# First x chunk turned on TensorE from a plain load, and wk spread over two queues, in place of DMA transposes for every x chunk and wk on one queue

## The chip, the cores and the metric

The kernel runs on one core of one Trainium2 chip. The metric is the device time of one execution in microseconds, the median of three runs. The profile is that of one execution, and its own time is given beside its span.

## The reference

Inputs are x (2048 rows of 640, bfloat16), the weights of two branches, and a gate vector. Branch A is a linear attention with 32 heads of 20, branch B a mixer with shifted groups and an MLP. The two are mixed row by row.

```python
def _A_ref(x, wqkv, wo):
    qkv = (x @ wqkv) split into q, k, v of 32 heads x 20
    phi = lambda t: jnp.where(t > 0, t + 1, jnp.exp(t)) + 1e-6
    pq, pk = phi(q), phi(k)
    kv = jnp.einsum("bhsd,bhse->bhde", pk, v)
    z = jnp.einsum("bhsd->bhd", pk)
    num = jnp.einsum("bhqd,bhde->bhqe", pq, kv)
    den = jnp.einsum("bhqd,bhd->bhq", pq, z)[..., None] + 1e-6
    return (num / den) in rows of 640 @ wo

def _B_ref(x, w1, w2, w3, w4):
    h = _gelu(_layernorm(x) @ w1)
    hs = (four column groups of h shifted by 1, -1, 2, -2 rows) @ w2
    x1 = x + hs
    return x1 + _gelu(_layernorm(x1) @ w3) @ w4

g = _sigmoid((x * gate_w).sum(-1, keepdims=True))
out = g * a + (1 - g) * b
```

## The kernel before

The 2048 rows are 16 chunks of 128 (NCH), or 4 tiles of 512 (NT). The 640 columns are 5 slices of 128 (DC). The order of work on every engine is the program's order: the kernel is written out by hand in stages, and no scheduler moves anything.

The stages in order: K (`k_mm`, `k_evac`, lines 184 to 221), one chunk at a time, 5 slices by 2 halves of the columns; Q (`q_unit`, L228); G, the product of phi(k) with x (`g_unit`, L303), with the statistics and scaling of the first layernorm on VectorE; the first B product (`w1_unit`, L337), the attention's small matrices, den (L239 to L250); then, tile by tile, the second B product (L408), attention (L439), w3 (L455) and w4 (L472).

K needs x transposed: `xT` holds x with its columns on the partitions, 5 slices by 2048. Before the change all of it is made by DMA transposes straight from memory (`load_xT`, L121), eight of them, on SP's queue, for chunks 0, 1, 2, 3, 4-5, 6-7, 8-11 and 12-15. Behind them on the same queue stand the loads of wq, of the untransposed `x_sb` (`load_x`, L118) and of all other weights. K's weights `wk_sb` come in 5 slices of 128 rows (`load_wk`, L124), 160 KB each, all on ACT's queue, with the small gate vector `g5` (L128) behind the first.

The column 640 of `wk_sb` is the gate vector: it arrives as 5 rows of 128, is turned on TensorE (L206) and copied by VectorE (L207), so that K's second half gives the gate's logit as a 321st column.

TensorE begins with products of ones (`warmup`, L200), first 6 of 512 columns and 2 of 128, then g's transpose, then 4 of 128. K's first two chunks are interleaved so that each slice of wk is used by both: chunk 0 takes slices 0, 1, 2, each followed by a product of ones of 256 columns; chunk 1 takes slices 0, 1, 2; then both take slice 3, then slice 4. From chunk 2 on each chunk takes its five slices in a row.

`k_evac` copies the gate's logit on ACT (L192) and forms phi: exp on ACT (L180), then two instructions on VectorE (L181, L182) that write `pk`.

PSUM is one pool of four buffers of two banks each (`pair`). A K chunk takes one, and so do the products of ones together with g's transpose.

Of the kernel before, what the change touches and what calls it, by code (L numbers as in the profile page):

```python
# [9 lines left out]
BF16 = mybir.dt.bfloat16  # L10
# [6 lines left out]
def kernel(  # L17
# [13 lines left out]
    nc = tc.nc  # L31
    P = 128
    S, D = A_x.shape[1], A_x.shape[2]
    F = B_w3.shape[1]
    H, Dh = 32, 20
    NCH = S // P
# [3 lines left out]
    DC = D // P  # L40
    HD = D // 2
# [27 lines left out]
    def pair():  # L69
        return ps.tile([P, 2, 512], F32, name="pp")  # L70


    x_sb = const.tile([P, NCH, D + 2], BF16)
# [12 lines left out]
    ident = const.tile([P, P], BF16)  # L86
    g5 = const.tile([DC, P], BF16)
# [19 lines left out]
    wk_sb = st1.tile([P, DC, D + 16], BF16)  # L107
    gT = wk_sb
    xT = st1.tile([P, DC, S], BF16)
# [5 lines left out]
    sp, aq, gq = nc.sync, nc.scalar, nc.gpsimd  # L115

    def load_x(c0, c1):
        sp.dma_start(x_sb[:, c0:c1, 0:D], x2[c0 * P:c1 * P, :].rearrange("(c p) d -> p c d", p=P))  # L118

    def load_xT(c0, c1):  # L120
        sp.dma_start_transpose(xT[:, :, c0 * P:c1 * P], x2[c0 * P:c1 * P, :])  # L121

    def load_wk(q, dc):
        q.dma_start(wk_sb[:, dc, 0:D], A_wqkv[dc * P:(dc + 1) * P, D:2 * D])  # L124

    load_wk(aq, 0)
    load_xT(0, 1)
    aq.dma_start(g5[:], gate_w.rearrange("(c p) -> c p", p=P))  # L128
    for dc in range(1, DC):
        load_wk(aq, dc)  # L130
    for c0, c1 in ((1, 2), (2, 3), (3, 4), (4, 6), (6, 8), (8, 12), (12, 16)):
        load_xT(c0, c1)
    sp.dma_start(wq_sb, wqkv_v[:, :, 0:D])
    load_x(0, 8)
    load_x(8, 12)
    load_x(12, 16)
    sp.dma_start(wv_sb[:], wqkv_v[:, :, 2 * D:3 * D])
# [37 lines left out]
    def phi(dst, src, n):  # L175
        e = e_p.tile([P, 1024], BF16, name="e")
        ev = e[:, 0:n]
        if len(src.shape) == 3:
            ev = ev.rearrange("p (h e) -> p h e", h=src.shape[1])
        nc.scalar.activation(ev, src, ACT.Exp)  # L180
        nc.vector.tensor_scalar(e[:, 0:n], e[:, 0:n], 1.0, 1e-6, op0=ALU.min, op1=ALU.add)  # L181
        nc.vector.scalar_tensor_tensor(dst, src, 0.0, ev, op0=ALU.max, op1=ALU.add)  # L182

    def k_mm(pt, c, dcs, hfs=(0, 1), last=DC - 1):
        for dc in dcs:
            for hf in hfs:
                n = HD + hf
                nc.tensor.matmul(pt[:, hf, 0:n], lhsT=xT[:, dc, c * P:(c + 1) * P],  # L188
                                 rhs=wk_sb[:, dc, hf * HD:hf * HD + n], start=(dc == 0), stop=(dc == last))

    def k_evac(pt, c):
        nc.scalar.copy(ylog[:, c:c + 1], pt[:, 1, HD:HD + 1])  # L192
        phi(pk[:, c, :].rearrange("p (h e) -> p h e", h=2), pt[:, :, 0:HD], D)
# [4 lines left out]
    def warmup(n, w=TS):  # L198
        for i in range(n):
            nc.tensor.matmul(warm[:, 1, 0:w], lhsT=one[:, 0:P], rhs=one[:, 0:w], start=True, stop=True)  # L200

    warmup(6)
    warmup(2, P)
    kp = [pair(), pair()]
    tg = warm[:, 0, :].bitcast(BF16)
    nc.tensor.transpose(tg[:, 0:DC], g5[:], ident[0:DC, 0:DC])  # L206
    nc.vector.tensor_copy(wk_sb[:, :, D], tg[:, 0:DC])  # L207
    warmup(4, P)
    for dc in range(3):
        k_mm(kp[0], 0, (dc,))  # L210
        warmup(1, 2 * P)
    k_mm(kp[1], 1, (0, 1, 2))
    for c in range(2):
        k_mm(kp[c], c, (3,))
    for c in range(2):
        k_mm(kp[c], c, (4,))
        k_evac(kp[c], c)
    for c in range(2, NCH):
        pt = pair()
        k_mm(pt, c, range(DC))  # L220
        k_evac(pt, c)
# [364 lines left out]
```

## Time and profile before

| | |
|---|---|
| time before, median of 3 runs | 268.53 us (268.37 to 268.89) |
| the profiled execution's own time | 268.89 us |
| its span, first to last instruction | 267.2 us |
| granted TensorE clock, mean | 0.997 |
| TensorE busy | 260.6 us (98%) |
| K stage from 9.35 to 29.13 us | 144 of its 160 products |

Times inside the profile count from the start of its span. In the page's first part each engine has its busy time, its share of the span and the number of its instructions. The chain of waits lists, in order of time, the work that the end depended on: start, length, and what it was. In the timeline a line is a run of like instructions: start, length, engine, line, operation, what it writes and reads, how many; in brackets the idle time of the engine before it and what ended it. A line of the DMA view gives what is moved, the queue that issues it, how many, their size, and the time from issue to landing. Matmul ends are modelled, so the step from one start to the next tells more than a single length.

### The profile page before, as it was taken

To read this page: it belongs to the slowest core of one execution; us is meant where nothing else is said; L and a number is where in the kernel's file an instruction comes from. 1 tells how busy PE (TensorE), PEld (TensorE's weight loads), DVE (VectorE), ACT (ScalarE), POOL (GpSimd) and SP (SyncE) were. 2 spreads that over 40 slices of the span, in tenths; PEclk is the share of its full clock that TensorE was granted. 3 is DMA by queue.
4 is the path that set the end of the run, shared out by engine and by line. 5 is a ranking of instruction groups with operands and counts; after the bars stand their busy time and mean duration, and the time that the engine had idled before them with its cause. 6 is when DMAs were issued, how large, how long until landed. Compare 5 with 4: busy or idle time off the path is not lost.

```text
span 267.2 us, 4246 instructions
## 1 busy us (share of the span) xinstructions
PE 260.6 (98%) x1738; PEld 162.2 (61%) x1738; DVE 138.5 (52%) x268; ACT 84.2 (32%) x122; POOL 20.4 (8%) x55
## 2 busy tenths in 40 slices
PE   7899999999999999999999999999999999999994
PEld 3677655688854654556567556567565566455662
DVE  0398778799948497864502464503454413122032
ACT  1455444411164716713330212340222340333100
POOL 7100010012220041001000001000001000000000
PEclk9999999999999999999999999999999999999998
DMA  7999988016676125800042000042000042000011
GB/s 147 210 209 367 374 258 319 0 27 123 123 96 125 29 42 98 305 2 0 15 86 76 25 0 2 0 98 76 25 0 2 1 98 76 25 0 2 0 61 37
DMA packets 46748, 23.77 MB, mean 89 GB/s; under 512 B 36106, under 2 KB 46090, under 8 KB 46730
## 3 DMA queue, kind: packets, MB, share of 16 engines
q1 hardware_dynamic: 46000, 22.70, 32.8%
q10 hardware_dynamic: 730, 0.82, 1.4%
q8 instruction: 13, 0.21, 0.3%
q14 instruction: 5, 0.04, 0.0%
HBM read 12.21 MB, written 2.62 MB: 56 GB/s over the span
## 4 chain that ended last, share of the span: by engine, by line
PE 92%; DMA 4%; DVE 2%; issue 0%; ACTq 0%; DVEq 0%
PE pp L472 21%; PE pp L455 21%; PE pp L303 8%; PE pp L408 8%; PE pp L439 8%; PE pp L228 8%; PE pp L188 7%; PE pp L337 6%; DMA wk_sb<-in_A_wqkv_dram 2%; DVE r_bf L250 1%; PE pp L460 1%; DMA lnxT<-ln 1%; PE pp L481 1%; PE pp L375 1%; DMA g<-in_gate_w_dram 1%; DVE hsT L347 0%
## 5 line engine op out<-in xcount | busy, mean ns | idle before, releaser
L455 PE MATMUL pp<-lnxT,w_sb 128*128 128x512 bf16 x260 | 60.4, 379 | 0.0
L463 ACT ACTIVATE h<-pp 128x1024 bf16<-128x1024 f32 (+1 forms) x28 | 27.8, 993 | 102.8 <-PE pp L455 94.4
L472 PE MATMUL pp<-w_sb,h 128*128 128x320 bf16 x416 | 57.9, 299 | 0.0
L472 PEld LDWEIGHTS <-h 128*128 128x128 bf16 x416 | 40.1, 98 | 17.0 <-issue 1.9
L455 PEld LDWEIGHTS <-w_sb 128*128 128x128 bf16 x260 | 25.4, 98 | 26.7
L488 DVE SCALAR_TENSOR_TENSOR oc<-pp,omg,x 128x640 bf16<-128x640 f32 x15 | 12.9, 881 | 44.0 <-PE pp L481 27.1
L442 DVE SCALAR_TENSOR_TENSOR x<-pp,gate,x 128x640 f32<-128x640 f32 x16 | 13.9, 868 | 29.4 <-PE pp L439 29.4
L411 DVE TENSOR_TENSOR x<-pp,x_sb 128x640 f32<-128x640 f32 x16 | 13.1, 820 | 22.9 <-PE pp L408 22.9
L180 ACT ACTIVATE e<-pp 128x640 bf16<-128x640 f32 (+1 forms) x26 | 21.5, 828 | 9.6 <-PE pp L228 9.6
L439 PE MATMUL pp<-m_sb,pqT 128*128 128x320 bf16 x160 | 24.3, 299 | 0.0
L188 PE MATMUL pp<-wk_sb,xT 128*128 128x320 bf16 (+1 forms) x160 | 23.1, 304 | 1.2 <-DMA wk_sb<-in_A_wqkv_dram 1.2
L408 PE MATMUL pp<-w_sb,hsT 128*128 128x320 bf16 x160 | 23.9, 299 | 0.0
L303 PE MATMUL pp<-x_sb,pk 128*128 128x320 bf16 (+1 forms) x160 | 22.3, 300 | 0.0
L228 PE MATMUL pp<-xT,hsT 128*128 128x512 bf16 x100 | 21.7, 379 | 0.0
L303 PEld LDWEIGHTS <-pk 128*128 128x128 bf16 x160 | 18.8, 117 | 3.5
L188 PEld LDWEIGHTS <-xT 128*128 128x128 bf16 x160 | 15.8, 99 | 7.9 <-issue 1.7
L408 PEld LDWEIGHTS <-hsT 128*128 128x128 bf16 x160 | 15.6, 98 | 8.2 <-issue 0.2
L439 PEld LDWEIGHTS <-pqT 128*128 128x128 bf16 x160 | 15.7, 98 | 7.7
L337 PE MATMUL pp<-lnxT,w_sb 128*128 128x512 bf16 x80 | 17.9, 379 | 0.0
L228 PEld LDWEIGHTS <-hsT 128*128 128x128 bf16 x100 | 11.8, 118 | 9.7
L273 POOL TENSOR_SCALAR rstd<-mv 128x4 f32<-128x4 f32 (+1 forms) x11 | 3.4, 313 | 157.2 <-DVE mv L279 157.2
L181 DVE TENSOR_SCALAR e<-e 128x640 bf16<-128x640 bf16 (+1 forms) x26 | 9.6, 368 | 11.2 <-ACT e L180 10.3
(73 smaller groups left out, 192.4 us busy)
## 6 DMA issues: line engine op xcount, KB each, us to landing
out_dram<-oc SPq DMA_DIRECT2D x15, 160.0 KB, 1.8
w_sb<-in_B_w_dram SPq DMA_DIRECT2D x1, 2160.0 KB
w_sb<-in_B_w_dram SPq DMA_DIRECT2D x1, 2080.0 KB, 10.3
x_sb<-in_A_x_dram SPq DMA_DIRECT2D x1, 1280.0 KB, 8.6
x_sb<-in_A_x_dram SPq DMA_DIRECT2D x2, 640.0 KB, 10.5
wo_sb<-in_A_wo_dram SPq DMA_DIRECT2D x6, 160.0 KB, 7.6
wk_sb<-in_A_wqkv_dram ACTq DMA_DIRECT2D x5, 160.0 KB, 3.8
hsT<-in_A_wqkv_dram SPq DMA_DIRECT2D x1, 800.0 KB, 5.6
```

Source lines behind the costliest of these rows:

```text
L180: nc.scalar.activation(ev, src, ACT.Exp)
L188: nc.tensor.matmul(pt[:, hf, 0:n], lhsT=xT[:, dc, c * P:(c + 1) * P], rhs=wk_sb[:, dc, hf * HD:hf * HD + n], start=(dc == 0), stop=(dc == ...
L228: nc.tensor.matmul(pt[:, t % 2, :], lhsT=wq_sb[:, dc, :].rearrange("p (m j) -> p j m", j=DC)[:, j], rhs=xT[:, dc, t * TS:(t + 1) * TS], st ...
L303: nc.tensor.matmul(pt[:, hf, 0:HD + hf], lhsT=w, rhs=x_sb[:, c, hf * HD:(hf + 1) * HD + hf], start=(c == 0), stop=(c == NCH - 1))
L337: nc.tensor.matmul(pt[:, i, :], lhsT=w, rhs=lnxT[t][:, dc, :], start=(dc == 0), stop=(dc == DC - 1))
L408: nc.tensor.matmul(pt[:, hf, 0:HD], lhsT=hsT[:, fc, 2 + c * P:2 + (c + 1) * P], rhs=w2_sb[:, fc, hf * HD:(hf + 1) * HD], start=(fc == 0), ...
L411: nc.vector.tensor_tensor(x1[:].rearrange("p (h e) -> p h e", h=2), pt[:, :, 0:HD], x_sb[:, c, 0:D].rearrange("p (h e) -> p h e", h=2), op ...
L439: nc.tensor.matmul(pt[:, hf, 0:HD], lhsT=pqT[:, j, c * P:(c + 1) * P], rhs=m_sb[:, j, hf * HD:(hf + 1) * HD], start=(j == 0), stop=(j == D ...
L442: nc.vector.scalar_tensor_tensor(x1, pt[:, :, 0:HD], gate[:, c:c + 1], x1, op0=ALU.mult, op1=ALU.add)
L455: nc.tensor.matmul(pt[:, k, :], lhsT=w3_sb[:, dc, fc * P:(fc + 1) * P], rhs=lnT[:, dc, :], start=(dc == 0), stop=(dc == DC - 1))
L463: nc.scalar.activation(h2[:, 2 * i * TS:2 * i * TS + n], pt[:].rearrange("p h e -> p (h e)")[:, 0:n], ACT.Gelu_apprx_tanh)
L472: nc.tensor.matmul(dst, lhsT=st[t]["h2"][:, fc * TS + cc * P:fc * TS + (cc + 1) * P], rhs=w4_sb[:, fc, a:b], start=start and fc == 0, stop ...
```

## The change

x chunk 0 is no longer transposed by DMA. It is loaded plainly into `x_sb`, first on SP's queue, and turned on TensorE in five transposes, two into one PSUM buffer and three into another; VectorE copies them into `xT`. g's transpose and copy stand between the two groups. The later `load_x(0, 8)` becomes `load_x(1, 8)`.

wk's slices 1 and 3 go on SP's queue, ahead of the DMA transposes; g, then slices 0, 2 and 4 on ACT's.

The products of ones ahead are 5 of 512 and 1 of 128 columns instead of 6 and 2; those behind g's copy are 5 of 128 instead of 4. K's chunk 0 is worked alone, its slices in the order 1, 0, 2, 3, 4, with a product of 256 columns of ones after each but the last; chunk 1 is worked like all later ones.

```diff
-    load_wk(aq, 0)
-    load_xT(0, 1)
-    aq.dma_start(g5[:], gate_w.rearrange("(c p) -> c p", p=P))
-    for dc in range(1, DC):
-        load_wk(aq, dc)
+    load_x(0, 1)
+    aq.dma_start(g5[:], gate_w.rearrange("(c p) -> c p", p=P))
+    load_wk(sp, 1)
+    load_wk(aq, 0)
+    load_wk(aq, 2)
+    load_wk(sp, 3)
+    load_wk(aq, 4)
     for c0, c1 in ((1, 2), (2, 3), (3, 4), (4, 6), (6, 8), (8, 12), (12, 16)):
         load_xT(c0, c1)
     sp.dma_start(wq_sb, wqkv_v[:, :, 0:D])
-    load_x(0, 8)
+    load_x(1, 8)
...
-    def k_mm(pt, c, dcs, hfs=(0, 1), last=DC - 1):
+    def k_mm(pt, c, dcs, first=0):
         for dc in dcs:
-            for hf in hfs:
+            for hf in range(2):
                 n = HD + hf
                 nc.tensor.matmul(pt[:, hf, 0:n], lhsT=xT[:, dc, c * P:(c + 1) * P],
-                                 rhs=wk_sb[:, dc, hf * HD:hf * HD + n], start=(dc == 0), stop=(dc == last))
+                                 rhs=wk_sb[:, dc, hf * HD:hf * HD + n], start=(dc == first), stop=(dc == DC - 1))
...
-    warmup(6)
-    warmup(2, P)
-    kp = [pair(), pair()]
+    warmup(5)
+    warmup(1, P)
+    kp = pair()
+    turns = [(pair()[:, 0, :].bitcast(BF16), a, b) for a, b in ((0, 2), (2, DC))]
     tg = warm[:, 0, :].bitcast(BF16)
-    nc.tensor.transpose(tg[:, 0:DC], g5[:], ident[0:DC, 0:DC])
-    nc.vector.tensor_copy(wk_sb[:, :, D], tg[:, 0:DC])
-    warmup(4, P)
-    for dc in range(3):
-        k_mm(kp[0], 0, (dc,))
-        warmup(1, 2 * P)
-    k_mm(kp[1], 1, (0, 1, 2))
-    for c in range(2):
-        k_mm(kp[c], c, (3,))
-    for c in range(2):
-        k_mm(kp[c], c, (4,))
-        k_evac(kp[c], c)
-    for c in range(2, NCH):
+    for n, (ptb, a, b) in enumerate(turns):
+        for dc in range(a, b):
+            nc.tensor.transpose(ptb[:, (dc - a) * P:(dc - a + 1) * P], x_sb[:, 0, dc * P:(dc + 1) * P], ident[:])
+        nc.vector.tensor_copy(xT[:, a:b, 0:P], ptb[:, 0:(b - a) * P].rearrange("p (c s) -> p c s", c=b - a))
+        if n == 0:
+            nc.tensor.transpose(tg[:, 0:DC], g5[:], ident[0:DC, 0:DC])
+            nc.vector.tensor_copy(wk_sb[:, :, D], tg[:, 0:DC])
+    warmup(5, P)
+    for n, dc in enumerate((1, 0, 2, 3, 4)):
+        k_mm(kp, 0, (dc,), first=1)
+        if n < DC - 1:
+            warmup(1, 2 * P)
+    k_evac(kp, 0)
+    for c in range(1, NCH):
         pt = pair()
         k_mm(pt, c, range(DC))
         k_evac(pt, c)
```

## The prediction

> **What bounds the kernel now.** I read the page first, then the chain of waits for the first 52 us, then the timeline and the DMA issues of the first 12 us, since the change touches nothing later.
>
> ```profile
> span 267.2 us, 4246 instructions
> PE 260.6 (98%) x1738; PEld 162.2 (61%) x1738; DVE 138.5 (52%) x268; ACT 84.2 (32%) x122; POOL 20.4 (8%) x55
> ```
>
> TensorE is busy in all but 6.6 us, so a gain must come out of those few us or out of work done at a slow clock. The chain shows where it starts:
>
> ```profile
> 1.20 2.35 DMA g<-in_gate_w_dram
> 3.54 0.02 issue
> 3.56 5.75 DMA wk_sb<-in_A_wqkv_dram
> 9.31 0.04 issue
> 9.35 19.78 PE pp L188 x144
> 29.13 21.58 PE pp L228 x100
> ```
>
> From 9.35 us the chain is TensorE alone, K products (L188), then Q products (L228), then nearly all the rest. Ahead of that it is DMA: the fifth slice of wk was issued at 3.56, the moment g landed, and took 5.75 us. (The kernel's DMAs share eight completion semaphores; wk's fourth and fifth slice take two that are in use. The fourth was issued at 3.09, when the first slice landed at 3.07.) The timeline shows TensorE before that:
>
> ```profile
> 4.15 0.58 PE L200 MATMUL pp<-const-bfloat16-1.0 128*128 128x128 bf16 x4 [0.27 <-DVE wk_sb L207]
> 4.53 0.74 PE L188 MATMUL pp<-wk_sb,xT 128*128 128x320 bf16 x2
> 5.06 0.42 PE L200 MATMUL pp<-const-bfloat16-1.0 128*128 128x256 bf16 x1
> 5.81 0.42 PE L200 MATMUL pp<-const-bfloat16-1.0 128*128 128x256 bf16 x1
> 6.76 0.43 PE L188 MATMUL pp<-wk_sb,xT 128*128 128x320 bf16 x2 [0.53 <-DMA wk_sb<-in_A_wqkv_dram]
> 7.03 0.27 PE L200 MATMUL pp<-const-bfloat16-1.0 128*128 128x256 bf16 x1
> 9.35 3.16 PE L188 MATMUL pp<-wk_sb,xT 128*128 128x320 bf16 x22 [0.69 <-DMA wk_sb<-in_A_wqkv_dram]
> ```
>
> Two things are to be seen. Products wait twice for wk. And the array runs slowly until about 6 us: a pair of 320-wide products takes one step of 0.53 (4.53 to 5.06) before, and 0.27 (6.76 to 7.03) after; the 256-wide one 0.42, then 0.27. The trace's clock record starts at 6.15.
>
> The DMA issues, each asked for in a stretch that holds one of them, are the first and fourth wk slice and the first and third transposed x chunk:
>
> ```profile
> wk_sb<-in_A_wqkv_dram ACTq DMA_DIRECT2D x1, 160.0 KB, 2.3
> wk_sb<-in_A_wqkv_dram ACTq DMA_DIRECT2D x1, 160.0 KB, 4.6
> xT<-in_A_x_dram SPq DMA_TRANSPOSE x1, 3.0
> xT<-in_A_x_dram SPq DMA_TRANSPOSE x1, 6.0
> ```
>
> With their issue times: wk lands at 3.1, 5.3, 6.7, 7.7, 9.3; x chunks 0, 1, 2, 3, 4-5, 6-7, 8-11, 12-15 at 3.8, 7.0, 9.4, 9.9, 11.2, 13.1, 16.5, 20.4. A plain 160 KB takes longer and longer because it shares the engines with transposes.
>
> **My yardstick** is the start of chunk 2. Before, it is 9.35 plus the four products left of chunks 0 and 1 (4 x 0.136) = 9.89. From there to 29.13 there are 14 chunks, 1.37 each. Everything later follows TensorE: Q's weights are issued at 16.9 and land 5.6 later, over five us before Q; x and the other weights have landed by 46, long before use at 50.6. The stretch where VectorE leads (79 to 87) counts from the end of G, so moves along. So the time changes by as much as chunk 2's start does.
>
> **Part by part, after the change.**
>
> x chunk 0 becomes a plain load, first on SP's queue. Its nearest row is wk's first slice: same bytes, first on its queue, 2.3. So it lands at 0.79 + 2.3 = 3.1; bounds 1.8 (the output stores) and 3.0 (the transposed chunk), 2.6 to 3.8. Warm-up: two products fewer ahead, one 512 wide (step 0.43) and one 128 wide (0.11). 0.83 + 5 x 0.43 + 0.11 = 3.1. Both end together.
>
> Five transposes of 128 columns, cold step 0.11. The first two issue from 3.15, the result stands at 3.15 + 0.11 + 0.31 (one isolated 128-wide product) = 3.57. VectorE copies 256 columns out of PSUM. From 0.18 for 5 columns (L207) to 0.82 for 640 (L182), 1.0 ns a column: 0.43, so 3.61 to 4.04. Then g's copy, 0.18, to 4.24. The other three transposes and their copy (384 columns, 0.56, to 4.8) lie beside products that need dc 1 and 0 alone. The five warm-ups behind them wait for g's copy, as L200 does at 4.15 above, so they start at 4.29; TensorE idles some 0.4 there instead of 0.27. They take 5 x 0.107. **K starts at 4.8** (before: 4.53; bounds 4.3 to 5.5 with x's landing).
>
> K of chunk 0, all slow: 5 x 0.53 + 4 x 0.22 (256-wide fillers) = 3.5, to 8.3. If the clock rises at 6.15 as before, 1.35 is done by then and the other 2.15 takes half: **chunk 0 ends at 7.2**, chunk 2 starts at 7.2 + 1.37 = **8.6**. No second chunk is worked beside it any more.
>
> wk now goes 1 and 3 on SP, 0, 2, 4 on ACT. Among the first eight DMAs none waits for a semaphore, so with 0.35 to 0.6 an issue all stand by 2.9 (g first, 0.75, delays wk 0 to 1.55). Six plain loads at 367 GB/s (the stretch 20 to 28) are 0.45 each; from the first bytes at about 1.7 that is 4.4, and about 5.5 where the first transposes share. They are wanted in the order 1, 0, 2, 3, 4 at 4.8, 5.5, 6.2, 6.5, 6.9. Covered; without that cover the old 9.3 would return. [...]
>
> x chunk 1's transpose now has three plain issues ahead on SP (3 x 0.43) in place of one transpose (1.32): 2.1 against 2.16. The whole SP queue behind it keeps its place. By bytes, six plain (2.7) and two transposed chunks at 0.98 (chunks 8 to 15 land 3.9 us apart by four) give 1.7 + 2.7 + 2.0 + 0.5 tail = 6.9 for chunk 2; wanted at 8.6. Bounds: 6.9 and the old 9.4; I take 7.5, since the old lateness was wk's. Chunks 3, 4, 6, 8 and 12 are wanted at 10.0, 11.3, 14.1, 16.8 and 22.3: in time even at the old landings.
>
> PSUM: chunk 0's buffer is free 2.3 after its last product (ACT 0.87, VectorE 0.33 + 0.82, gaps), too late for chunk 2 were it given that one. The two buffers of the transposes and the warm-up's come free earlier and should go first: nothing. ACT's table load (1.28) moves ahead with its shorter queue, hidden.
>
> Sum: 9.89 - 8.6 = 1.3 us off. The profiled execution took 268.89 (267.2 and 1.7 around it), 0.36 above the median; 268.53 - 1.3 = **267.2**. A tenth later in x's landing costs 0.05, as the rest of the wait is in the slow clock.
>
> **Rivals.** *The clock rises late.* Before, it rose 5.3 us after the first warm-up (0.83 to 6.15), over work with one gap of 0.27. Now five transposes and a 0.4 gap stand between 3.1 and 4.3. If the count starts anew at 4.29, the rise comes at 9.6; of the slow path to chunk 2 (4.8 + 3.5 + 2.67 = 11.0) the rest then takes half, 10.3: 0.4 slower, 268.9. If it stays low through chunk 1: 1.1 slower, 269.7. Break-even is a rise at 8.7; one at 9.8 makes 269.1. For it: the gap has grown and transposes may not do what products do. Against: fillers and products run unbroken from 4.3. Middle 269.3. [...]
>
> *The transposes deliver late.* SP's issue pace (1.31 a chunk) is untouched. If chunk 2 lands at the old 9.44, the gain is 0.45: 268.1.
>
> *The change doesn't do what it says*: chunk 2 gets chunk 0's buffer. Then it starts at 7.2 + 2.3 + 0.1 = 9.6: 268.2.
>
> **How the numbers follow.** A measurement here can tell about 0.2% (0.54 us) from no change. Forecast 0.5, own range 266.5 (the clock up by 4.8, when K starts: chunk 0 ends at 6.55, chunk 2 starts at 7.9) to 268.0 (x chunk 0 at its late bound and a clock half a us later). Late transposes or the buffer 0.18, nearly all within 0.2%. Late clock 0.3, most of it slower. The rest, 0.02, faster by another way. So faster 0.52, same 0.23, slower 0.25; range 266.5 to 269.6, which leaves out only the late clock's worst end and a little below.
>
> **What would show it.** Right: K's first product near 4.8, no wait for wk from then on, 0.27 a pair from about 6.2, chunk 2 near 8.6, Q near 27.8. Wrong: pairs of 0.53 beyond 8 us; a wait for xT at chunk 1 or 2; chunk 0's wait ended by a wk slice; or L228 moved and the span not, which would mean that a later stage was held by something other than TensorE.

## The result and the profile after

The changed kernel takes 267.70 us (median of four runs, 267.51 to 267.72) beside 268.57 for the kernel before on the same chip (four runs, 268.37 to 268.89). The ratio is 0.9965, 95% interval 0.9948 to 0.9982: faster, by 0.9 us. A second set, among the experiments below, gave 0.9940 (0.9921 to 0.9960), 1.3 us; the two intervals overlap. The forecast was 1.3 us and a time of 267.2.

The page of the profiled execution, which itself took 267.71:

```profile
span 266.0 us, 4258 instructions
PE 260.9 (98%) x1743; PEld 162.8 (61%) x1743; DVE 139.4 (52%) x270; ACT 84.3 (32%) x122; POOL 20.3 (8%) x55
```

TensorE's busy time is about the same (260.6 before), and 1.2 us of the span are gone. The chain of waits (start, length, what) shows where from:

```profile
0.83 2.40 PE pp L202 x6
3.23 0.26 PE pp L211 x2
3.49 0.12 PE pp L214
3.60 0.43 PE pp L211 x3
4.03 0.61 PE pp L202 x5
...
6.15 0.53 PE pp L190 x2
6.68 0.21 PE pp L202
6.89 0.27 PE pp L190 x2
7.16 0.11 PE pp L202
7.27 20.71 PE pp L190 x152
27.98 21.58 PE pp L232 x100
```

No DMA stands in it any more. TensorE works from 0.83 to the end of K without a wait: the products of ones (L202), the x transposes (L211), g's (L214), K's products (L190). What is left of the start is slow clock: a pair takes 0.53 at 6.15 and 0.27 at 6.89. Q begins at 27.98 by the chain, where it was 29.13. (The chain counts from modelled ends; the first Q product itself starts at 27.82, before at 28.97, and the table below goes by starts.)

The timeline of TensorE and of VectorE in the same stretch (idle time before, and what ended it, in brackets):

```profile
3.09 0.40 PE L211 MATMUL pp<-ident,x_sb 128*128 128x128 bf16 x2
3.53 0.50 PE L211 MATMUL pp<-ident,x_sb 128*128 128x128 bf16 x3
3.96 0.69 PE L202 MATMUL pp<-const-bfloat16-1.0 128*128 128x128 bf16 x5
4.44 0.74 PE L190 MATMUL pp<-wk_sb,xT 128*128 128x320 bf16 x2
3.52 0.29 DVE L212 COPY xT<-pp 128x256 bf16<-128x256 bf16 x1 [3.52 <-PE pp L211]
3.73 0.17 DVE L215 COPY wk_sb<-pp 128x5 bf16<-128x5 bf16 x1
4.07 0.36 DVE L212 COPY xT<-pp 128x384 bf16<-128x384 bf16 x1 [0.17 <-PE pp L211]
```

And the DMA issues of x chunk 0, of wk's last slice, and of x chunk 1's transposes, with the time to landing at the end:

```profile
x_sb<-in_A_x_dram SPq DMA_DIRECT2D x1, 160.0 KB, 2.3
wk_sb<-in_A_wqkv_dram ACTq DMA_DIRECT2D x1, 160.0 KB, 3.7
xT<-in_A_x_dram SPq DMA_TRANSPOSE x1, 4.5
```

Issued at 0.79, 2.25 and 2.18, they land at 3.0, 5.9 and 6.65. wk's last slice landed at 9.3 before.

### The profile page after: what moved, and what is told of

Read it like the earlier page. It is cut to its first block, busy times and chain, and to the rows that moved or that the text cites. A ratio compares the mean times of both kernels' runs of the same rounds, so it can differ in the third digit from the quotient of the medians.

```text
span 266.0 us, 4258 instructions
## 1 busy us (share of the span) xinstructions
PE 260.9 (98%) x1743; PEld 162.8 (61%) x1743; DVE 139.4 (52%) x270; ACT 84.3 (32%) x122; POOL 20.3 (8%) x55
## 4 chain that ended last, share of the span: by engine, by line
PE 95%; DVE 2%; DMA 1%; issue 0%; DVEq 0%
PE pp L476 22%; PE pp L459 21%; PE pp L190 8%; PE pp L307 8%; PE pp L412 8%; PE pp L443 8%; PE pp L232 8%; PE pp L341 6%; PE pp L202 1%; DVE r_bf L254 1%; PE pp L464 1%; DMA lnxT<-ln 1%; PE pp L485 1%; PE pp L379 1%; DVE hsT L351 0%; PE pp L360 0%
## 5 line engine op out<-in xcount | busy, mean ns | idle before, releaser
L182 ACT ACTIVATE e<-pp 128x640 bf16<-128x640 f32 (+1 forms) x26 | 21.5, 826 | 9.6 <-PE pp L232 9.6
L190 PE MATMUL pp<-wk_sb,xT 128*128 128x320 bf16 (+1 forms) x160 | 23.5, 306 | 0.0
L190 PEld LDWEIGHTS <-xT 128*128 128x128 bf16 x160 | 16.0, 100 | 6.3
```

## The experiments

My theory was that wk's last slices had been the bound, that the change brings them early by their place in the queues, and that the slow clock is the next limit. The rivals were that the turn on TensorE does it, or that the clock's rise or the DMA transposes take the gain back. Each run has a profile. The table puts them together: K's first product, the clock's rise (the first entry at full speed in the trace's clock record), the start of chunk 2, the landing of the transposes that hold chunk 8, and the first Q product (us, of the profiled execution), then the median and the ratio to the kernel before, measured beside it.

| kernel | K | rise | chunk 2 | chunk 8 landed | Q | median | ratio (95%) |
|---|---|---|---|---|---|---|---|
| before | 4.53 | 6.15 | 9.89 | 16.49 | 28.97 | 268.57 | |
| before, again | 4.53 | 6.38 | 10.09 | 16.55 | 29.17 | 269.03, one run | |
| changed | 4.44 | 6.76 | 8.74 | 16.44 | 27.82 | 267.70 | 0.9965 (0.9948-0.9982) |
| changed, again | 4.46 | 4.79 | 8.53 | 16.80 | 27.75 | 267.33 | 0.9940 (0.9921-0.9960) |
| split of wk only | 4.53 | 4.89 | 9.28 | 17.41 | 28.36 | 268.19 | 0.9990 (0.9974-1.0005) |
| turn only | 4.47 | 4.85 | 13.3 | 16.68 | 33.27 | 272.78 | 1.0143 (1.0118-1.0167) |
| no fillers | 4.37 | 4.10 | 8.08 | 16.36 | 27.32 | 267.30 | 0.9943 (0.9922-0.9963) |
| no front warm-up | 4.56 | 7.76 | 9.28 | 15.95 | 28.35 | 267.97 | 0.9974 (0.9957-0.9990) |
| split, chunk 0 alone | 4.52 | 4.55 | 8.79 | 17.80 | 28.75 | 268.48 | 0.9993 (0.9977-1.0009) |
| fillers doubled | 4.31 | 4.08 | 9.47 | 17.34 | 28.54 | 267.65 | 0.9956 (0.9940-0.9973) |
| longer front | 4.93 | 5.00 | 8.17 | 16.80 | 27.76 | 267.64 | 0.9954 (0.9939-0.9969) |
| split, alone, two by two | 4.53 | 5.30 | 8.92 | 15.42 | 28.18 | 267.74 | 0.9973 (0.9954-0.9992) |
| g on GpSimd's queue | 6.30 | 9.65 | 11.0 | 16.78 | 30.08 | 269.21 | 1.0021 (1.0002-1.0041) |
| no fillers, two by two | 4.50 | 4.98 | 8.03 | 14.00 | 27.24 | 267.09 | 0.9935 (0.9918-0.9952) |

From the first Q product to the end of the span all fourteen profiles take 237.8 to 238.3 us. So the start decides, as the yardstick supposed. One profile is one execution: the kernel before scatters from 267.7 to 270.0 over the comparisons, so the medians and the ratios carry the verdicts and the profile the reasons.

**Split of wk only.**

```diff
-    for dc in range(1, DC):
-        load_wk(aq, dc)
+    load_wk(sp, 1)
+    load_wk(aq, 2)
+    load_wk(sp, 3)
+    load_wk(aq, 4)
```

> The kernel before with one part of the change: wk slices 1 and 3 go on SP's queue behind chunk 0's DMA transpose, 0, 2, 4 stay on ACT's; chunk 0 is still transposed by DMA, warm-ups and order of products as before. My theory: the late wk slices were the whole bound, and what cures them is where they stand in the queues (all among the first eight DMAs, ahead of x chunk 1's transpose). Then wk's last slice lands by 6.5 us, chunk 2 starts at about 8.9 and the time is about 267.7. Rival: the turn on TensorE is what matters, since chunk 0's DMA transpose holds both SP's queue (1.3 us) and the DMA engines: then wk's last slice lands at 8.5 or later, chunk 2 starts at 9.5 or later, and the time is 268.2 or more.

wk's last slice landed at 6.60, close to what the place in the queues was to give, but chunk 2 started at 9.28, between the two. The chain names the next in line:

```profile
3.19 0.04 issue
3.23 4.08 DMA xT<-in_A_x_dram
7.31 0.05 issue
7.36 21.17 PE pp L190 x154
```

x chunk 1's transposes, pushed back on SP's queue by two plain loads (issue at 3.23 instead of 2.16), are now waited for, and chunk 0's slices 3 and 4 stand behind that wait in the order of products. For wk the split did more than save issue time: the slice that landed last was issued 0.8 us earlier than before (2.77 for 3.56) and landed 2.7 earlier (6.60 for 9.31), with x chunk 1's transposes now issued behind it. The split alone is worth no more than the interval can tell.

**Turn only.**

```diff
-    load_wk(sp, 1)
-    load_wk(aq, 0)
-    load_wk(aq, 2)
-    load_wk(sp, 3)
-    load_wk(aq, 4)
+    for dc in (1, 0, 2, 3, 4):
+        load_wk(aq, dc)
```

> The changed kernel with wk back on ACT's queue alone, in the order of use 1, 0, 2, 3, 4 behind g; chunk 0 turned on TensorE. The fifth slice shares a completion semaphore with the first and is issued only when that has landed. My theory (place in the queues decides): the fifth slice is issued near 3.5 to 4, lands at 8 to 9, chunk 2 starts at 9.2 to 9.6 and the time is about 268.1. Rival (the turn decides, by taking one transposed chunk out of the DMA engines' way): the fifth slice lands by 6.9, chunk 2 starts at 8.7 and the time is 267.7, that of the changed kernel.

The last slice was issued at 4.00, as expected of the queues, and landed at 9.8, later than expected; the turn alone does not free wk. The time I missed by 4.7 us, for a reason that neither theory had. TensorE's waits (in total, times, longest), and the products that they delayed:

```profile
PE pp L187 <- DMA wk_sb<-in_A_wqkv_dram: 3.1, 2, 1.6
6.81 0.43 PE L187 MATMUL pp<-wk_sb,xT 128*128 128x320 bf16 x2 [1.60 <-DMA wk_sb<-in_A_wqkv_dram]
9.43 0.69 PE L187 MATMUL pp<-wk_sb,xT 128*128 128x320 bf16 x2 [1.45 <-DMA wk_sb<-in_A_wqkv_dram]
```

These waits were for the second and the fourth slice (issued at 1.77 and 2.74, landed at 6.77 and 9.38), not for the fifth. Each of the two was issued right behind the slice before it; x chunk 1's transposes had been issued ahead of both, at 1.25. And the stretches 4.9 to 8.2, 8.3 to 15 and 15.1 to 20: length, then the busy times of TensorE, its weight loads, VectorE, ACT and GpSimd, the granted clock, the DMA share and GB/s:

```profile
4.90:8.20 3.30, 1.39 (x9) 0.68 (x7) 0.00 (x0) 0.76 (x1) 2.27 (x8) 1.00 1.16 196
8.30:15.00 6.70, 5.58 (x22) 3.18 (x22) 1.67 (x4) 1.53 (x4) 0.00 (x0) 0.50 1.14 223
15.10:20.00 4.90, 4.90 (x38) 3.50 (x36) 3.44 (x7) 2.46 (x8) 0.00 (x0) 1.00 0.92 197
```

TensorE was busy for 1.39 of 3.30 us, with the whole first wait and the start of the second in it, and the clock fell to half for 6.8 us. The two late slices cost their waits, 3.1 us, and the stretch at half clock followed.

**No fillers.**

```diff
         k_mm(kp, 0, (dc,), first=1)
-        if n < DC - 1:
-            warmup(1, 2 * P)
```

> The changed kernel without the four 256-wide products of ones between chunk 0's slices. My theory: after the change no wk slice is waited for, so they only lengthen the slow stretch, by 0.21 each; K starts at 4.44 as in the changed kernel, five slices take 5 x 0.53 at the slow clock, chunk 0 ends at 6.9 instead of 7.4, chunk 2 starts at 8.25 instead of 8.74, time 267.2. Rival: chunk 1's or 2's DMA transposes then become the limit (chunk 1's landed at 6.65 in the changed kernel), or the third slice of wk (5.42) is waited for and the clock rises later: time 267.7 or more.

The median is that of my theory within 0.1, but the profile does not bear its reason out: the clock had risen at 4.10, before K, so there was no slow stretch to shorten. K then waited 0.66 for wk's third slice and began chunk 1 at 6.71, as x chunk 1 landed at 6.66.

**No front warm-up.**

```diff
-    warmup(5)
-    warmup(1, P)
```

> The changed kernel without the products of ones ahead of the transposes (5 of 512 and 1 of 128 columns); the five of 128 behind the transposes stay. My theory (the rise follows TensorE's own work): TensorE starts at 3.1 instead of 0.83, the clock rises at 8.4 or later (5.3 to 5.9 us after the first work, as in the two profiles), chunk 2 starts at 9.5 to 10.2 and the time is 268.5 to 269.2. Rival: the rise comes at a set time of the execution whatever ran before, at 6.2 to 6.8 us: chunk 2 starts at 8.7 and the time stays at 267.7.

In the profile the rise is late, at 7.76, and K is slow to there; chunk 2 starts at 9.28, earlier than I had worked out. The median, 267.97, lies between the two expectations, the runs from 266.97 to 268.55. That the rise follows the work fits this one profile. By the medians the front (the products of ones ahead) is worth 0.3 to 0.6 us, not over one; by the ratios, 0.9974 against 0.9965 and 0.9940 with overlapping intervals, its worth is not told apart from nothing.

**The changed kernel again**, unaltered.

> The changed kernel once more, unaltered, to see what its time owes to the moment of the clock's rise, which lay between 4.10 and 7.76 us in the profiles so far. My theory: that moment is chance (it falls on the edge of a 3.41 us period that is not tied to the program's start), and sets chunk 0's end as long as it lies behind K's start at 4.44: chunk 2 starts at 1.37 + half of (rise + 7.96), and not before 8.1. The runs then scatter between 267.0 and 267.9. Rival: the rise belongs to the kernel: 6.76 again, chunk 2 at 8.74, and a scatter of 0.2 as in the first four runs (267.51 to 267.72).

The 3.41 us of the theory is the length of the turn-only kernel's first stretch at full speed, from 4.85 on. Here the rise came at 4.79 and chunk 2 started at 8.53 and not at 8.1: wk's third slice was waited for 0.3 us, and x chunk 1's transposes, which landed at 7.12 this time, 0.3 more. The six runs scatter from 266.7 to 267.9, so the narrow scatter of the first set does not belong to the kernel.

**Split, chunk 0 alone.** The split-only kernel with this edit:

```diff
-    for dc in range(3):
-        k_mm(kp[0], 0, (dc,))
-        warmup(1, 2 * P)
-    k_mm(kp[1], 1, (0, 1, 2))
...
-    for c in range(2, NCH):
+    for dc in range(DC):
+        k_mm(kp, 0, (dc,))
+        if dc < DC - 1:
+            warmup(1, 2 * P)
+    k_evac(kp, 0)
+    for c in range(1, NCH):
```

> The kernel with the split of wk alone (chunk 0 still transposed by DMA), now with chunk 0 worked alone as in the changed kernel, slices in the order 0 to 4. In the split-alone run TensorE stood 0.64 us waiting for x chunk 1 while chunk 0's slices 3 and 4 lay ready behind it in the order. My theory: this order uses that wait, chunk 1 starts when its transposes land at 7.3, chunk 2 starts at 8.7 and the time is 267.7: split and order give all of the gain and the turn on TensorE nothing. Rival: the turn is needed: as the split alone, chunk 2 at 9.3, 268.2.

Half of my theory held: chunk 2 at 8.79, as in the changed kernel. The time did not follow. The chain says where the gain was given back:

```profile
10.45 7.34 DMA xT<-in_A_x_dram
17.80 0.05 issue
17.84 11.07 PE pp L190 x80
```

One DMA delivers chunks 8 to 11, and chunk 8 waits 0.7 for it. With chunk 0's transposes still on SP's queue, all later ones are issued later (10.45 against 9.87 in the changed kernel). So the theory "the turn gives nothing" fell as put, and the next run tests its successor.

**The same, chunks 8 to 11 by two DMAs.**

```diff
-    for c0, c1 in (..., (6, 8), (8, 12), (12, 16)):
+    for c0, c1 in (..., (6, 8), (8, 10), (10, 12), (12, 16)):
```

> The kernel with wk's split, chunk 0 transposed by DMA and worked alone, now with chunks 8 to 11 transposed by two DMAs of two chunks instead of one of four. That kernel had chunk 2 at 8.8, but then stood 0.7 us waiting for chunks 8 to 11, which a single DMA delivers at 17.8. My theory: chunks 8 and 9 now land by 16.8, the wait goes or is under 0.2, and the time is 267.7 to 268.0: what the turn on TensorE buys is earlier delivery behind it on SP's queue, and not the start. Rival: the queue as a whole is too slow without the turn; the wait comes back at chunk 10 or 12, and the time stays at 268.3 or more.

Chunks 8 and 9 land at 15.4, and the time is 267.74. No wait for `xT` stands among TensorE's waits any more, up to 30 us; chunk 4 alone begins 0.2 later than the even step of 1.36 would have it:

```profile
PE pp L202 <- PEq L568: 0.8, 1, 0.8
PE pp L190 <- DMA wk_sb<-in_A_wqkv_dram: 0.5, 1, 0.5
PE pp L202 <- DVE wk_sb L209: 0.3, 1, 0.3
```

Without any turn of x on TensorE this is not told apart from the changed kernel (0.9973 against 0.9965 and 0.9940, intervals that overlap). Its interval also overlaps that of the kernel without this last edit (0.9993, 0.9977 to 1.0009), so it is the wait gone from the profile that carries the reading: what the turn buys is delivery further down SP's queue, and that can be had there directly. One thing stays open. Three of the twelve runs took 269.3 to 269.5, and none of the changed kernel's ten took more than 267.94; no such run was profiled, so whether the turn also guards against them is not known.

**Fillers doubled.**

```diff
-            warmup(1, 2 * P)
+            warmup(2, 2 * P)
```

> The changed kernel with two 256-wide products of ones behind each of chunk 0's first four slices instead of one. My theory: nothing is waited for there, so each lies on the path, 0.21 while the clock is low and 0.11 after: 0.4 to 0.6 longer, 268.2. Rival: they lie in waits for wk, and cost nothing: 267.7.

0.3 above the changed kernel's second set, below its first: not told apart. In the profile (its slowest run, 268.54) wk's third slice landed at 6.81 and was waited for 1.4 us, which is the rival's case.

**Longer front.**

```diff
-    warmup(5)
-    warmup(1, P)
+    warmup(6)
+    warmup(2, P)
```

> The changed kernel with the old number of products of ones ahead of the transposes (6 of 512 columns and 2 of 128, instead of 5 and 1). My theory: x chunk 0 has landed at 3.04, so the front's longer end (3.6 instead of 3.03) delays turn and K by 0.5; half of it is in the time where the clock rises after K's start, all of it where it rises before: 0.3 to 0.5 longer, 268.1. Rival: the longer front makes up for it by a sooner rise of the clock: 267.7 or less.

K starts 0.5 later, as expected. It cost 0.3 against the second set and nothing against the first, so it is not told apart either. In the profile the later start did not show: the clock rose at 5.00, no wk slice was waited for, chunk 2 began at 8.17, and then chunk 8 waited for its transposes:

```profile
9.51 7.29 DMA xT<-in_A_x_dram
16.80 0.05 issue
16.85 11.07 PE pp L190 x80
```

**The kernel before again**, unaltered.

> The kernel before once more, unaltered, for a second profile. My theory: the same wait decides whatever the moment of the clock's rise: wk's fifth slice lands at 9.0 to 9.6, chunk 2 starts at 9.6 to 10.2, and from the first Q product on everything takes 238.0 as in all ten profiles so far (237.8 to 238.3). Rival: the clock's rise moves this kernel too, by more than 0.5.

```profile
1.19 2.28 DMA g<-in_gate_w_dram
3.48 0.04 issue
3.52 5.99 DMA wk_sb<-in_A_wqkv_dram
9.51 0.04 issue
9.55 19.78 PE pp L188 x144
```

The same two DMAs, one behind the other, end at 9.51. The rise lay at 6.38, only 0.23 from the first profile's, so the rival on the clock was hardly tested.

**g on GpSimd's queue**, the kernel before with one word changed.

```diff
-    aq.dma_start(g5[:], gate_w.rearrange("(c p) -> c p", p=P))
+    gq.dma_start(g5[:], gate_w.rearrange("(c p) -> c p", p=P))
```

> The kernel before with g's small load issued from GpSimd's queue instead of ACT's. wk's slices then are issued one behind the other, and none waits for g's landing; all stay on ACT's queue, and all DMA transposes stay where they were. My theory: wk's lateness has two parts, the late issue (3.09 and 3.56 for the last two) and the transposes it shares the engines with. With the last issued near 3.1 at the latest it lands at 8.0 to 8.8, chunk 2 starts at 8.8 to 9.4, time 268.0 to 268.3. Rival one: the late issue is all: it lands by 7.0, chunk 2 at 8.7, time 267.7. Rival two: the sharing is all: it lands at 9.2 or later as before, and the time is 268.6.

wk's slices 1 to 4 were issued 0.3 to 0.9 us earlier than before, and the last, issued at 3.22, landed at 8.07 instead of 9.3. The issue itself, 0.34 us earlier for the last slice, is one part of the lateness; nearly five us from issue to landing remain, beside the transposes. The two parts are not cleanly separated, since x chunk 0's transposes landed later in this run (5.67 for 3.77). The time answers another question, since g itself came late by this queue, as TensorE's timeline shows:

```profile
5.47 0.18 PE L206 MATMUL pp<-ident,g 5*128 5x5 bf16 x1 [1.71 <-DMA g<-in_gate_w_dram]
```

From its chain:

```profile
8.00 0.53 PE pp L188 x2
8.54 0.21 PE pp L200
```

TensorE stood 1.7 us for g, and the clock rose at 9.65 only: pairs still take 0.53 at 8.0. This is the loss that the late-clock rival priced, brought about by accident. Chunk 2 starts at 11.0, 1.1 later than before.

**No fillers, two by two**: both edits on the changed kernel.

> The changed kernel without the four products of ones between chunk 0's slices, and with chunks 8 to 11 transposed by two DMAs of two chunks. Without the fillers alone, chunk 2 started at 8.1 and chunk 8 waited 0.15 for its transposes (landed at 16.4). My theory: both limits are eased, Q starts at 27.2 instead of 27.8 and the time is 267.1, the lowest of all. Rival: chunk 1's transposes (6.7 to 7.1) and the wait for wk's third slice hold the start, and delivery the rest: 267.3, no different from the changed kernel run again.

Q starts at 27.24 and the median is 267.09, as expected and the lowest of all. Against the kernel before it is 0.65% (0.48 to 0.82). Against the changed kernel, 0.9940 in its second set, it is not told apart by these runs. What ends its start is x chunk 1 again:

```profile
2.17 4.44 DMA xT<-in_A_x_dram
6.61 0.05 issue
6.66 20.75 PE pp L190 x150
```

## Why the prediction was right

The mechanism was the forecast's: wk's waits go, K runs from its first product on, the slow clock is next, and all after it moves along. In the profiles chunk 2's start went from 9.89 to 8.74 and Q's from 28.97 to 27.82, 1.15 both; 1.3 were forecast. The first set's medians say 0.9 because the profiled execution of before was its slowest run of four; the second set says 1.3. That is also where most of the miss in the time lies (267.70 for 267.2): the sum took a saving worked out from an execution of 268.89 off the median of 268.53, which is 0.36 lower. Taken off 268.89 it gives 267.6, and the changed kernel's profile took 267.71.

The terms, in order. x chunk 0's landing: 3.1 forecast, 3.04 measured. The end of the front: 3.1, 3.09. **K's start: 4.8 forecast, 4.44 measured.** Here a term was mis-sized: 1.0 ns a column, taken from L207 and L182, made 0.43 of the copy of 256 columns; it took 0.29, and that of 384 columns 0.36, so 0.5 ns a column. L182 (0.82 for 640 columns) reads 32-bit values and forms two operations on them, and was not the nearest row that it seemed. With the copies short, TensorE's gap of 0.4 shrank to about 0.1, and the products of ones behind it began at 3.96 instead of 4.29. **The clock's rise: 6.15 taken over from before, 6.76 measured**, which made the start 0.3 longer. Chunk 0's end was 7.38 by the products (7.2 forecast). The two errors nearly cancel, by luck: chunk 2 at 8.74 for 8.6.

wk: the slices landed at 4.2 to 5.9 in the first profile (about 5.5 forecast for the last), none waited for. In the second the third slice came at 5.82 and was waited for 0.3, so the cover is thinner than I wrote. x chunk 1 landed at 6.65 and 7.12. The late-transposes rival, given a small chance, was half there: in the second profile chunk 1 waits 0.3 (its logit follows chunk 0's by 1.64 us instead of 1.36), and chunk 8's logit, whose transposes landed at 16.80, follows chunk 7's by 1.50 instead of 1.36, a wait of 0.14. The sentence that fell is "in time even at the old landings": it took 16.49 as a fixed number, and chunk 8 landed between 16.0 and 17.8 in the kernels with a single DMA for it. In each of these that had chunk 2 before 9 us, chunk 8 waited, or had 0.5 us to spare at most.

The buffer rival did not occur: chunk 2 began at 8.74, 1.36 after chunk 1's start, without a wait for a buffer.

The late-clock rival did not occur in the changed kernel, and its mechanism as put, a count of 5.3 us that starts anew behind a gap, is doubtful. In the kernel before the rise came 2.0 us behind the end of a gap of 0.27 (4.15 to 6.15), and with g on GpSimd's queue 4.2 behind the end of one of 1.71 (5.47 to 9.65). In the trace's clock records the stretches at full speed last 259.41 or 262.83 us, 3.42 apart, outside the turn-only kernel; in that one the clock rose for 3.41 and fell for 6.83. In all fourteen profiles TensorE is, by the modelled ends, busy for 92% or more of the 3.41 us ahead of the rise, and for 74% or less of the 3.41 us before those. Whether transposes do for the clock what products do, which this rival doubted, the runs do not decide. With the transposes left out, the lowest share ahead of a rise is 73% (fillers doubled, no fillers just above it), and the highest in the 3.41 us before those is 70% (the changed kernel, to 3.34 us). Either way of counting puts all shares ahead of a rise above all the others, and no run varied the transposes alone.

What decides the size of the gain now is therefore several limits close together: the clock's rise, wk's third slice, x chunk 1's transposes and chunk 8's. Each held TensorE back in some profile. That would explain why taking the fillers out, doubling them or lengthening the front moved the median by 0.4 at most; it was not tested further.

## What to carry to other kernels

Where the chain of waits starts with a DMA, look at what holds its issue and what shares its way, and put the loads that are needed first ahead of all transposes (in the changed kernel wk's last slice then landed at 5.92 instead of 9.31): here the order in the queues, together with chunk 0 worked alone and one large transpose cut in two, reached the changed kernel's median, and the change of engine was worth what it took out of the queue. A DMA that delivered four chunks made the first wait for the last (chunk 8 landed at 17.80, and at 15.42 by one of two chunks); cut it where the consumer arrives early. A gain at the start was paid out only until the next delivery (chunk 2 at 8.79 for 8.74, but Q at 28.75 for 27.82 behind the wait for chunk 8), so work out the landings behind it with their scatter, not with one profile's number.

## What the hardware showed that I had not expected

The clock's rise lies anywhere between 4.1 and 6.8 us in the kernels where TensorE works from 0.83 on without a long wait before it (7.8 without the front, 9.7 behind the wait for g), so one profile's rise is no term for a sum. In the turn-only kernel the clock also fell again after 3.41 us at full speed, of which the stretch 4.9 to 8.2 had TensorE busy for 1.39 of 3.30 us. That cost some 2.8 us (an estimate: half of the 5.58 us that TensorE was busy from 8.3 to 15.0).

The DMA engines moved transposed chunks at little more than half the rate of plain loads. In the changed kernel the stretches 12 to 20 us (transposes, with plain loads in its last part) and 20 to 27 us (plain loads), with the GB/s at the end:

```profile
12.00:20.00 8.00, 8.00 (x61) 5.76 (x59) 6.73 (x13) 4.46 (x13) 0.00 (x0) 1.00 1.04 208
20.00:27.00 7.00, 7.00 (x53) 5.00 (x52) 5.95 (x11) 4.04 (x12) 0.00 (x0) 1.00 1.06 369
```

The engines are full in both (1.04 and 1.06), the rates 208 and 369.
